# The low half of a reloaded weight piece, given to VectorE one unit later

## The chip, the cores and the metric

One core of one Trainium2 chip runs the whole program, one launch. The metric is device time in microseconds (us) of one execution; lower is better.

## What is computed

Three blocks follow one another, all in 32-bit floats. First attention over 2 x 8 heads of 768 tokens with 64 columns, in which a query sees only keys of its own hash bucket:

```python
q_bits = (np.einsum('bhsd,dk->bhsk', q, proj) > 0).astype(np.int64)
k_bits = (np.einsum('bhsd,dk->bhsk', k, proj) > 0).astype(np.int64)
...
mask = q_bucket[:, :, :, None] == k_bucket[:, :, None, :]
scores = np.where(mask, scale * np.matmul(q, k.transpose(0, 1, 3, 2)), -1000000000.0)
attn = np.exp(scores - np.max(scores, axis=-1, keepdims=True))
attn = attn / (np.sum(attn, axis=-1, keepdims=True) + 1e-09)
return np.matmul(attn, v).astype(np.float32)
```

Then a gated feed-forward block, `((x @ w1) * (x @ w2)) @ w3 @ w_out` on 1536 tokens of 512 columns (hidden width 1024), and at the end a layer of 8 experts, of which each token uses the one with the largest gate logit: `gate * (relu(x @ w1[e]) @ w2[e])`.

## The kernel before

The matmuls want more precision than one pass gives, so most operands are held as two numbers, a high part (rounded by a copy on ScalarE) and a low part (the rest, a subtraction on VectorE or GpSimd), and three products are summed (`TERMS`). The high part must be there before the low part can be taken.

The attention is written as a loop over units, `for i in range(NU + LEAD + NLAG + 1)` with `NU` = 96, and the order of the instructions of every engine is the order in which the loop emits them. Unit i does, in this order: `stage_1(units[i])` for i under 96 (two score matmuls, L343, and the row maximum of these scores on VectorE, L350, read from PSUM); the transpose of the finished maxima when a half is complete (`stage_f`, L361, with a copy `rT` on ScalarE and two small writes by SP, L366); whatever was put off to this unit (`todo_at`, filled by `after(n, fn)`, run at L861); `stage_a`, the product with v (L392); `stage_2` for unit i - 9 (four score matmuls, L378, the exponential on ScalarE, L379, and the running sum of the exponentials on GpSimd, `acc`, L384); from unit 98 on half a feed-forward step of the next block (`moe_half`, L682); and at the very end of the unit `flush()`, which emits what lies in `misc`. `stage_1` and `stage_2` draw their PSUM tiles from one tag, `s`, with two buffers; which of the two a tile gets is settled when the program is built, and a tile's first matmul waits until the buffer's last reader is through. A unit from 92 on also begins with `norm_step` (`x_t`'s high part by a ScalarE copy, L638, and its low part by VectorE one unit later, L640).

The weights w1 and w2 were written to DRAM earlier, as 16 pieces of 128 x 512 (`wfd`), and come back from unit 84 on through a ring of five buffers, `st`. In `order` they have the numbers k = 40 to 55. A piece is split by `split`: ScalarE copies its high part to `hi` (L494) and VectorE subtracts, `lo = T - hi` (L495). For k from 40 on, both are emitted by `flush()` at the end of the unit, followed by `nxt()`, which asks for the load of piece k + 5 into the same buffer two units later (`after(2, ...)`, L467 on SP). By `RATE2` the pieces 40 to 45 are flushed in the units 91 to 96, one each, 46 and 47 in unit 97, 48 to 53 in the units 98 to 103, and 54 and 55 in unit 104. The first `moe_half`, in unit 98, reads the high and the low parts of the pieces 40, 42, 44 and 46.

Of the kernel before, what the change touches and what calls it, by code (L numbers as in the profile page):

```python
# [8 lines left out]
F32 = mybir.dt.float32  # L9
# [31 lines left out]
READY = 84  # L41
NST = 5
LEAD = 9
NDVE = 0
AGE = 2
NLAG = 4
RUN = 2
# [118 lines left out]
def body(tc, qT, kT, vP, w1d, w2d, w3d, wod, mod, wgate, mbias, e1, e2, cst, out):  # L166
    nc = tc.nc
    PE, ACT, DVE, POOL, SP = nc.tensor, nc.scalar, nc.vector, nc.gpsimd, nc.sync
# [28 lines left out]
    def ps(tag, shape, name):  # L197
        return psum[0].tile(shape, F32, tag=tag, name=name, bufs=nbuf.get(tag, 1))
# [248 lines left out]
    dq, misc, begun = [], [], set()  # L447

    def piece_load(k):
        i = order[k]  # L450
        if k in raws:
            return
        if i < 8:
            src = wod[i * P:(i + 1) * P, :]
        elif i < 24:
            f, hf = divmod(i - 8, 2)
            src = w3d[f, :, hf * 4:hf * 4 + 4, :].rearrange("p g f -> p (g f)")
        else:
            m, j = divmod((i - 24) % 16, 8)
            c, hf = divmod(j, 2)  # L460
            src = ((w1d, w2d)[m] if i < 40 else wfd[m])[c * P:(c + 1) * P, hf * 512:hf * 512 + 512]
        if i < 40:
            raws[k] = r_cr([P, 1024])
            SP.dma_start(raws[k].bitcast(I64), src)
        else:
            raws[k] = r_st([P, 512])
            SP.dma_start(raws[k], src)  # L467

    def piece(k):
        i = order[k]  # L470
        raw = raws[k]
        if i < 8:
            hi, lo = wo[:, 0, i, :], wo[:, 1, i, :]
        elif i < 24:
            f, hf = divmod(i - 8, 2)
            if hf == 0:
                w3_t[f] = r_w3([P, 2, 8, P], F32R)
            hi, lo = (w3_t[f][:, x, hf * 4:hf * 4 + 4, :].rearrange("p g f -> p (g f)") for x in range(2))
        elif i >= 40:
            m, j = divmod(i - 40, 8)  # L480
            c, hf = divmod(j, 2)
            hi, lo = (w12[m][:, x, c, hf * 512:hf * 512 + 512] for x in range(2))

        def nxt():
            ahead = k + (3 if k < 40 else NST)
            if ahead < (40 if k < 40 else 56):
                if k < 40:
                    piece_load(ahead)
                else:
                    after(2, lambda: piece_load(ahead))  # L490
            done["n"] += 1

        def split(T):
            ACT.copy(hi, T)  # L494
            (POOL if NDVE <= k < 40 else DVE).tensor_sub(lo, T, hi.bitcast(F32))  # L495

        if i >= 40:
            return [lambda: misc.append(lambda: (split(raw), nxt()))]
        T, t1 = r_T([P, 512]), ps("u", [P, 512], f"u{k}").bitcast(I32)
        w = raw.bitcast(I32).rearrange("p (n two) -> p n two", two=2)  # L500

        def last():
            DVE.scalar_tensor_tensor(T.bitcast(I32), w[:, :, 0], 29, t1, ALU.logical_shift_right, ALU.bitwise_or)
            if i < 24:
                misc.append(lambda: (split(T), nxt()))
            else:
                m, j = divmod(i - 24, 8)
                c, hf = divmod(j, 2)
                SP.dma_start(wfd[m][c * P:(c + 1) * P, hf * 512:hf * 512 + 512], T)
                misc.append(nxt)  # L510

        return [
            lambda: DVE.tensor_scalar(t1, w[:, :, 1], 3, 0x3FFFFFF8, ALU.logical_shift_left, ALU.bitwise_and),
            lambda: DVE.scalar_tensor_tensor(t1, w[:, :, 1], -0x40000000, t1, ALU.bitwise_and, ALU.bitwise_or),
            last,
        ]

    def fill():
        if dq and isinstance(dq[0], int):
            dq[0:1] = piece(dq[0])  # L520
        if dq:
            dq.pop(0)()
# [42 lines left out]
    def after(n, fn):  # L565
        todo_at.setdefault(slot[0] + n, []).append(fn)
# [567 lines left out]
    for i, k in enumerate((1, 2, 4, 8)):  # L1134
        nxt = inc[i % 2]
# [410 lines left out]
```

## Time and profile before

| | |
|---|---|
| runs | 687.93, 692.60, 692.66 us; median 692.6 |
| the profiled execution, its own time | 686.77 us |
| its span in the profile | 685.0 us |
| TensorE busy (matmul) | 653.3 us, 95% of the span |
| VectorE, ScalarE, GpSimd busy | 391.7, 313.2, 329.4 us |
| granted TensorE clock | 0.998 |

The profile is of one execution, with times counted from the start of its span; 1.8 us of the execution's time lie outside of it. PE is TensorE's matmul, DVE is VectorE, ACT is ScalarE, POOL is GpSimd, and SP issues the DMAs. L350 is line 350 of the kernel. In a timeline, what stands in brackets is the engine's idle time ahead of the row and the work whose end finished it.

### The profile page before, as it was taken

What the parts mean: (1) busy time and instruction counts of PE and PEld (TensorE: products, weight loads), DVE (VectorE), ACT (ScalarE), POOL (GpSimd) and SP (SyncE); (2) the same over time, 40 slices, a digit from 0 to 9 for tenths busy, and PEclk for the clock granted to TensorE, in tenths of its full rate; (3) what the DMA queues carried; (4) which work ended last, traced back from release to release, by engine and by line L of the source; (5) the groups of instructions that cost most, each with busy time, mean ns of one, the idle gap of its engine ahead of it and who ended that gap; (6) DMA issues with size and microseconds to landing.
All of it is one profiled execution on the core that took longest, in us unless ns stands there. A gap on an engine that the chain in (4) does not pass through costs nothing. (4 is left out here: it accounts for less than half of the span.)

```text
span 685.0 us, 11038 instructions
## 1 busy us (share of the span) xinstructions
PE 653.3 (95%) x4038; PEld 512.0 (75%) x4038; DVE 391.7 (57%) x606; ACT 313.2 (46%) x534; POOL 329.4 (48%) x323
## 2 busy tenths in 40 slices
PE   7998899999999897899999999999999999999995
PEld 2544666676667654578989898989888899899984
DVE  6788768676786997753632121121275775575550
ACT  7266474655555544553422122221224665565551
POOL 7499987787768576665524233231215222111110
PEclk9999999999999999999999999999999999999999
DMA  8747372736557555303201010100036887766630
GB/s 223 229 147 212 126 236 87 228 139 161 168 149 200 147 190 159 100 32 96 65 17 47 16 47 16 47 1 32 1 119 235 288 293 237 243 198 218 203 121 20
DMA packets 41692, 94.04 MB, mean 137 GB/s; under 512 B 6352, under 2 KB 12032, under 8 KB 41632
## 3 DMA queue, kind: packets, MB, share of 16 engines
q1 hardware_dynamic: 39552, 86.72, 40.9%
q0 software_dynamic: 2080, 6.56, 2.7%
q8 instruction: 34, 0.56, 0.3%
q14 instruction: 26, 0.21, 0.1%
HBM read 72.98 MB, written 12.94 MB: 125 GB/s over the span
## 5 line engine op out<-in xcount | busy, mean ns | idle before, releaser
L682 PEld LDWEIGHTS ab<-x,w 128*128 128x128 f32 x1152 | 140.5, 191 | 7.9 <-DVE w L495 2.4
L682 PE MATMUL ab<-x,w 128*128 128x256 f32 x1152 | 143.9, 284 | 2.6 <-DVE w L495 1.6
L384 POOL TENSOR_TENSOR acc<-acc,pt 128x770 f32<-128x770 f32 x64 | 119.4, 1865 | 17.6 <-ACT pt L379 12.4
L379 ACT ACTIVATE pt<-s 128x768 f32<-128x768 f32 x96 | 78.0, 813 | 97.3 <-PE s L378 89.9
L350 DVE TENSOR_REDUCE nm<-m 128x1 f32<-128x768 f32 x96 | 91.3, 954 | 52.6 <-PE m L343 52.4
L378 PEld LDWEIGHTS s<-q,k 128*128 128x128 f32 (+1 forms) x384 | 64.0, 189 | 42.4 <-issue 20.2
L693 POOL TENSOR_TENSOR g<-gf,g 128x256 fp32r<-128x256 f32 x48 | 35.3, 736 | 124.8 <-ACT g L692 119.4
L378 PE MATMUL s<-q,k 128*128 128x384 f32 (+1 forms) x384 | 91.5, 360 | 2.2 <-ACT pt L379 1.2
L1212 DVE TENSOR_TENSOR eu<-er,eu 128x1024 fp32r<-128x1024 f32 x56 | 68.1, 1233 | 25.0 <-ACT eu L1211 23.8
L392 PE MATMUL a<-pt,v 128*64 128x385 f32 x384 | 76.5, 504 | 0.0
L1401 POOL DMA_INDIRECT out<-o,sidx x13 | 14.7, 1131 | 121.6 <-ACT o L1400 105.6
L691 DVE TENSOR_TENSOR gf<-asb,ab 128x256 f32<-128x256 f32 x48 | 20.2, 420 | 92.7 <-ACT asb L690 92.4
L1375 PE MATMUL e1F<-ex,eu 128*128 128x256 f32 x576 | 70.3, 283 | 0.5 <-DVE ex L1341 0.3
L1375 PEld LDWEIGHTS e1F<-ex,eu 128*128 128x128 f32 x576 | 69.8, 190 | 1.4 <-DVE ex L1341 0.5
L1393 PE MATMUL e2F<-eu,h 128*128 128x512 f32 x288 | 69.0, 395 | 0.1
L1211 ACT CAST eu<-er 128x1024 fp32r<-128x1024 f32 x56 | 57.6, 1046 | 10.2 <-DMA er<-e 10.1
L1393 PEld LDWEIGHTS e2F<-eu,h 128*128 128x128 f32 x288 | 53.2, 188 | 11.6 <-DVE h L1380 0.5
L343 PE MATMUL m<-k,q 78*128 78x384 f32 x192 | 51.9, 353 | 10.0 <-DVE nm L350 6.8
L1011 PE MATMUL x2p<-w,g 128*128 128x512 f32 x240 | 58.1, 396 | 0.0
L596 PE MATMUL w<-wo,w 128*128 128x512 f32 x192 | 51.3, 400 | 1.9 <-ACT ev L599 1.6
L1011 PEld LDWEIGHTS x2p<-w,g 128*128 128x128 f32 x240 | 44.2, 188 | 11.4 <-issue 2.1
L690 ACT COPY asb<-ab 128x256 f32<-128x256 f32 x48 | 17.9, 372 | 72.2 <-PE ab L682 72.2
(202 smaller groups left out, 810.7 us busy)
## 6 DMA issues: line engine op xcount, KB each, us to landing
er<-e SPq DMA_DIRECT2D x56, 512.0 KB
cr<-w3d SPq DMA_DIRECT2D x16, 512.0 KB
cr<-wod SPq DMA_DIRECT2D x8, 512.0 KB
cr<-w1d SPq DMA_DIRECT2D x8, 512.0 KB
wfd<-cT SPq DMA_DIRECT2D x16, 256.0 KB
cr<-w2d SPq DMA_DIRECT2D x8, 512.0 KB
st<-wfd SPq DMA_DIRECT2D x16, 256.0 KB
raw<-kT SPq DMA_DIRECT2D x8, 384.0 KB
```

What stands on the lines that cost most here:

```text
L343: PE.matmul(s[:, half, 0:HS], q[0:KROWS[hd], 0, qt * P:qt * P + P], k[0:KROWS[hd], 0, half * HS:half * HS + HS], start=True, stop=True,)
L350: DVE.tensor_reduce(nm[:, 3 * hd + qt % 3:3 * hd + qt % 3 + 1], s[:, :, 0:HS], AX.XY, ALU.max, negate=True)
L378: PE.matmul(s[:, hd, 0:HS], k[0:n, i, c * P:c * P + P], q[0:n, i, cl], start=(i == 0), stop=(i == 1))
L379: ACT.activation(pts[j % NP][:, :, 0:HS], s[:, :, 0:HS], AF.Exp, scale=SCALE)
L384: POOL.tensor_add(acc, pts[(j - 1) % NP] if c == 1 else acc, pts[j % NP])
L392: PE.matmul(a_t[p, half][64 * hd:64 * hd + 64, :], v[:, c, 64 * hd:64 * hd + 64], pts[j % NP][:, hd, :], start=(c == 0), stop=(c == QT - 1 ...
L682: PE.matmul(ab[:, j, :], w12[j][:, st, c, fs], x[:, mv, c, :], start=(c == 0 and i == 0), stop=(c == 3 and i == 2))
L1011: PE.matmul(st["ps"], g_t[ch][:, a, f, i * P:i * P + P], w34[b][:, f, :], start=(f == 0 and k == 0), stop=(f == 7 and k == 2),)
L1211: ACT.copy(t[:, 0, sl], raw)
L1212: DVE.tensor_sub(t[:, 1, sl], raw, t[:, 0, sl].bitcast(F32))
L1375: PE.matmul(o[f], w[:, st, c, fs], x[:, mv, c, :], start=(c == 0 and i == 0), stop=(c == 3 and i == 2))
L1393: PE.matmul(o, h[:, st, f, sl], w[:, mv, f, :], start=(f == 0 and k == 0), stop=(f == 7 and k == 2))
```

## The change

For the pieces with k from 40 on, only the ScalarE copy is still emitted at the end of the unit. The VectorE subtraction, and behind it `nxt()`, go through `after(1, ...)`, so they are emitted in the next unit, behind `stage_1` and `stage_f` of that unit and ahead of its `stage_a`. `nxt()` counts its two units from there, so the request for the next load is emitted one unit later too. The constant `NDVE` goes, and the earlier pieces stay with GpSimd as before.

```diff
-NDVE = 0
...
         def split(T):
             ACT.copy(hi, T)
-            (POOL if NDVE <= k < 40 else DVE).tensor_sub(lo, T, hi.bitcast(F32))
+            POOL.tensor_sub(lo, T, hi.bitcast(F32))
 
         if i >= 40:
-            return [lambda: misc.append(lambda: (split(raw), nxt()))]
+            def later():
+                DVE.tensor_sub(lo, raw, hi.bitcast(F32))
+                nxt()
+
+            return [lambda: misc.append(lambda: (ACT.copy(hi, raw), after(1, later)))]
```

## Rows read from the trace of the kernel before

**Rows 1.** Page, busy time of each engine, with share and instructions.

```profile
PE 653.3 (95%) x4038; PEld 512.0 (75%) x4038; DVE 391.7 (57%) x606; ACT 313.2 (46%) x534; POOL 329.4 (48%) x323
```

**Rows 2.** Five stretches: length, busy us of each engine, PE clock, DMA share, GB/s.

```profile
core 0: us, PE busy (x) PEld busy (x) DVE busy (x) ACT busy (x) POOL busy (x), PEclk, DMA share, GB/s
263.86:285.64 21.78, 16.71 (x86) 8.72 (x85) 16.49 (x16) 13.33 (x24) 13.34 (x11) 1.00 0.36 98
276.31:278.80 2.49, 2.38 (x16) 0.84 (x14) 2.21 (x4) 2.04 (x5) 1.01 (x3) 1.00 0.36 105
285.95:309.00 23.05, 23.05 (x150) 17.32 (x150) 13.08 (x13) 12.07 (x23) 13.02 (x10) 1.00 0.17 58
309.00:520.00 211.00, 210.00 (x1523) 189.76 (x1522) 70.01 (x202) 54.80 (x135) 68.87 (x92) 1.00 0.15 47
520.00:670.00 150.00, 149.37 (x955) 134.53 (x955) 89.21 (x115) 82.90 (x126) 27.58 (x25) 1.00 0.67 226
```

**Rows 3.** Timeline of PE, units 92 to 98: start, duration, engine, line, tiles.

```profile
263.86 0.51 PE L343 MATMUL m<-k,q 78*128 78x384 f32 x2
...
266.96 0.62 PE L343 MATMUL m<-k,q 128*128 128x384 f32 x2 [0.90 <-ACT pt L379]
...
270.61 0.62 PE L343 MATMUL m<-k,q 78*128 78x384 f32 x2 [1.26 <-DVE nm L350]
...
273.89 0.62 PE L343 MATMUL m<-k,q 128*128 128x384 f32 x2 [0.96 <-ACT pt L379]
...
279.07 0.28 PE L361 MATMUL f<-ident,nm 128*12 128x128 f32 x1 [0.38 <-POOL nm L357]
...
285.64 0.38 PE L682 MATMUL ab<-x,w 128*128 128x256 f32 x1 [1.56 <-DVE w L495]
```

**Rows 4.** Timeline of VectorE, units 91 to 98.

```profile
265.61 1.85 DVE L495 TENSOR_TENSOR w<-st,w 128x512 fp32r<-128x512 f32 x1 [2.69 <-ACT w L494]
267.38 0.95 DVE L350 TENSOR_REDUCE nm<-m 128x1 f32<-128x768 f32 x1
268.25 1.44 DVE L495 TENSOR_TENSOR w<-st,w 128x512 fp32r<-128x512 f32 x1
269.61 0.94 DVE L350 TENSOR_REDUCE nm<-m 128x1 f32<-128x768 f32 x1
270.80 0.69 DVE L495 TENSOR_TENSOR w<-st,w 128x512 fp32r<-128x512 f32 x1 [0.24 <-ACT w L494]
271.41 0.42 DVE L640 TENSOR_TENSOR x<-xT,x 128x256 fp32r<-128x256 f32 x1
...
276.55 0.94 DVE L350 TENSOR_REDUCE nm<-m 128x1 f32<-128x768 f32 x1
...
281.27 2.07 DVE L640 TENSOR_TENSOR x<-xT,x 128x256 fp32r<-128x256 f32 x1
283.27 2.32 DVE L495 TENSOR_TENSOR w<-st,w 128x512 fp32r<-128x512 f32 x1
```

**Rows 5.** Timeline of GpSimd, the running sums of the units 91, 92 and 95 to 98.

```profile
265.07 4.07 POOL L384 TENSOR_TENSOR acc<-acc,pt 128x770 f32<-128x770 f32 x2 [1.60 <-ACT pt L379]
...
278.98 8.29 POOL L384 TENSOR_TENSOR acc<-acc,pt 128x770 f32<-128x770 f32 x4
```

**Rows 6.** Timeline of ScalarE, units 92, 98 and 99.

```profile
266.10 0.81 ACT L379 ACTIVATE pt<-s 128x768 f32<-128x768 f32 x1 [0.52 <-PE s L378]
...
283.59 0.61 ACT L494 CAST w<-st 128x512 fp32r<-128x512 f32 x1
287.82 0.81 ACT L379 ACTIVATE pt<-s 128x768 f32<-128x768 f32 x1 [3.61 <-PE s L378]
```

**Rows 7.** Timeline of SP's DMA issues, units 95 to 98.

```profile
276.31 0.32 SPq L467 DMA_DIRECT2D st<-wfd  x1
...
280.28 1.40 SPq L366 DMA_DIRECT2D q<-rT  x2
281.78 0.34 SPq L467 DMA_DIRECT2D st<-wfd  x1
```

## The prediction

> **What bounds the kernel now.** The engines' busy times come first: TensorE has 653.3 us of work in a span of 685.0, every other engine under 400 [rows 1]. So only a change that shortens TensorE's idle time counts, and the table by stage says where it idles. From the unit 92 to the first feed-forward half in unit 98 it works 16.71 of 21.78 us, so 5.07 us are lost; behind that it works 23.05 of 23.05, then 210.00 of 211.00 and 149.37 of 150.00 [rows 2]. A microsecond won before 285.95 us is therefore not waited away later: nothing there shows an end that another engine or a DMA sets.
>
> The timeline of PE names the five places [rows 3]: the scores of unit 93 wait 0.90 us for an exponential, those of unit 94 wait 1.26 for a maximum, those of unit 95 wait 0.96 for an exponential, the transpose of the maxima waits 0.38 for GpSimd, and the first half step waits 1.56 for the low part of piece 46. Together 5.06. The reader should see that three of them come from one cause, which stands on VectorE [rows 4]. The scores of unit 92 are ready at 263.86 + 0.51 = 264.37, but ahead of their maximum stands the subtraction of piece 40, for whose high part VectorE idles 2.69 us; it ends at 267.46, and the maximum runs only at 267.38. The same goes on: the maximum of unit 93 stands behind the subtraction of piece 41, which ends at 269.69. A late maximum keeps its PSUM buffer. That the scores of the units 93 and 95 wait for an exponential means that they were given the other buffer of the two, the one that `stage_2` has just used; the exponential of unit 92 ends at 266.10 + 0.81 = 266.91 [rows 6], and the scores of 93 start at 266.96.
>
> **The change, part by part.** Nothing is added or taken away: the same 16 copies, 16 subtractions and 11 loads run. What differs is the order on two queues.
>
> VectorE. The order changes for few pieces only. There is no maximum after unit 95, so only the subtractions of pieces 40 to 43 (flushed in the units 91 to 94) move behind one. Those of 42 to 45 also move behind one L640, 0.42 us where nothing disturbs it [rows 4]. From piece 46 on, no VectorE instruction stands between the old place and the new one: cost nothing, gain nothing. The maximum of unit 92 then starts at 264.4 and ends at 265.4, since it takes 0.95; the subtraction of 40 starts where it did, as its high part comes no sooner. So the scores of unit 93 can follow the matmuls of unit 92 directly, at about 265.9 in place of 266.96. I take it that the tile gets the buffer that comes free first, which is now the maximum's; the other case is a rival below. The maximum of 93 follows the subtraction of 40 at 267.4 and ends at 268.4, where it ended at 270.55; the scores of 94 start at about 268.4 in place of 270.61. By the same steps those of 95 start at about 271.1 in place of 273.89. Of the three waits, 3.12 us, I leave 0.2 for 94 and 0.4 for 95: 2.5 us won. The 0.38 at the transpose goes as well if the last maximum leads the additions by enough; I count between 0 and 0.4. TensorE thus reaches the half step 2.5 to 2.9 us sooner.
>
> The 1.56 us there are the doubtful term. Behind the last maximum (276.55 + 0.94 = 277.49) VectorE now has five subtractions up to piece 46, which ends at 285.59 [rows 4]; with the change it has six, because piece 43 moves behind that maximum. What one costs depends on GpSimd: undisturbed 0.69, but 1.85 at 265.61 and 2.32 at 283.27, each while a running sum was under way, and four sums back to back took 8.29, that is 2.07 each [rows 4, 5]. The 1.85 fit a sum that began at 265.07 and left VectorE its turn only after it. The Trainium skill, page "SBUF — State Buffer", section "Who interferes with whom", states it as a rule: a VectorE instruction with two SBUF inputs and a GpSimd instruction that reads SBUF exclude one another for the whole instruction, and whichever starts first goes first. The trace agrees: 2.07 for an L640 that takes 0.42 alone. By that rule the moved subtractions are no dearer in themselves, but each that meets a sum waits for its end; without it six subtractions would take the 0.69 or 0.42 of an undisturbed one and the 1.56 would be gone.
>
> So I follow the chain with one subtraction let in per sum. The last maximum ends between 273.0 (L640 ahead of it runs at once) and 274.8 (it waits for a sum of 1.8). Three or four subtractions fit before the sums of unit 95 and later begin, and one or two must pass between sums. Piece 46 then ends between 280.3 (soonest, by its copy on ScalarE) and 283.8. VectorE's own work in the stretch, 16.49 us from 264.4 on, gives 280.9 as a floor [rows 2]. TensorE wants it at 284.08 less 2.5 to 2.9, so about 281.4. The gain at 285.64 is then between 1.8 and 4.2 us; with the middle, 282.6, it is 3.0, and I take that.
>
> SP. The load of piece k + 5 is emitted a unit later, but an issue waits on its buffer, not on the unit: the load goes out when the subtraction of piece k is done. It matters only where something else on SP's queue comes between. The load of piece 45 now stands behind the two loads of `rb`, which wait for nothing new: nothing. The load of piece 48 stood ahead of the two rT writes (276.31) and now stands behind them, as that of 49 does before, at 281.78 [rows 7]. Its data needed 2.49 us, 105 GB/s over the stretch, which is its 0.26 MB [rows 2]. Shifted 3 us with the rest it goes out at about 278.8 and lands at 281.3; its copy ran at 283.59 and would now be due at about 280.6. So ScalarE may stand 0.7 us, and what is queued behind it is an exponential that waited 3.61 us for its scores [rows 6]: hidden. If that cover were gone it would cost 0.7. The `st` ring counts as empty one unit later, in unit 106 in place of 105, and the buffer that needs its room is first drawn in unit 107: nothing.
>
> ScalarE's order is the same, and so is GpSimd's. The sum: 2.5 to 2.9 from TensorE's waits, 0.1 to 0.5 from the half step, so 3.0. Against the profiled execution, 686.77 becomes 683.8 (span 682.0); it ran 5.8 us under the median of the runs, so on the median the forecast is 692.6 - 3.0 = 689.6 us.
>
> **Rivals.** (1) The tile keeps the exponential's buffer. Then the scores of 93 still start at 266.96, and of the three waits only the one on the maximum goes, 1.26 us, the rest being paid at the half step: 692.6 - 1.3 = 691.3. For it: the assignment before has it so at two of three units. Against it: the maximum would now be the earlier reader by 1.5 us. (2) The half step swallows all. Its wait ends with piece 46, and if the six subtractions take as long as the five did and the copy time that was idle, that end stays at 285.6: 692.6. For it: VectorE is busy 16.49 of 21.78 us there, more than ScalarE [rows 2]. Against it: its largest gap, 2.69, is exactly what the change fills. (3) Slower. The sixth subtraction falls into the row of sums, and all six have to wait for one: 6 x 2.07 = 12.4 us behind the last maximum. The point is 285.6 - 12.4 = 273.2: if that maximum ends later, the half step starts later than before. At 274.8 this costs 1.6 us, at the old 277.5 it costs 4.3; with the middle, 3.0, the time is 695.6. Against it: the sums resume at 278.98, 1.5 us behind the last maximum [rows 4, 5], which is room for two undisturbed subtractions. (4) All 5.06 go, 687.5, if the sums and the subtractions happen to miss each other.
>
> **How the numbers follow.** Forecast 0.60, rival (1) 0.17, (2) 0.10, (3) 0.08, (4) 0.05. The runs shown lie 4.7 us apart, 0.7%, so about 1% is what a measurement of this kernel can tell from no change. No case moves the time by 1%: 3.0 us are 0.4%, 4.3 are 0.6%. So faster by over 1% needs the gain and a median that falls among the lower runs, 0.11; slower by over 1% needs rival (3) and the reverse, 0.05; within 1% is 0.84. The range goes from 683, the profiled execution less 3 and a little, since a median may as well fall there, to 694, which takes in (1), (2) and the low end of (3).
>
> **What would show it.** In the profile after: the maximum of unit 92 at about 264.4, before the subtraction of piece 40, and no 2.69 us gap ahead of the latter; scores of the units 93 to 95 with less than 0.7 us of waits together; the first half step's wait for L495 between 0 and 2.4 us; work as without gaps behind it. The prediction is wrong if a wait of `stage_2` for a PSUM buffer takes the place of those of `stage_1`, if exponentials begin to wait for the running sums, or if a later stage shows new TensorE gaps.

## The result

| | median (lowest to highest) | runs | profiled: time, span, clock |
|---|---|---|---|
| before | 692.63 (687.93 to 694.10) | 4 | 686.77, 685.0, 0.998 |
| changed | 682.73 (680.84 to 682.87) | 4 | 682.61, 680.8, 0.995 |

The changed kernel takes 0.986 of the time of before, interval 0.9818 to 0.9903: faster by 1.4%, under the range that was given. The two profiled executions, however, differ by 4.2 us only, the medians by 9.9. Both have to be explained.

The stage from the scores of unit 92 to the end of the first half step, after the change (length, busy us of each engine, PE clock, DMA share, GB/s), and the stretches behind it:

```profile
265.10:281.88 16.78, 16.25 (x87) 8.89 (x86) 13.23 (x16) 12.84 (x23) 12.51 (x10) 1.00 0.32 90
281.88:309.00 27.12, 26.12 (x175) 19.56 (x175) 15.60 (x16) 13.84 (x27) 16.14 (x12) 1.00 0.23 72
309.00:520.00 211.00, 211.00 (x1520) 190.64 (x1520) 69.66 (x199) 53.65 (x132) 69.25 (x92) 1.00 0.16 50
520.00:670.00 150.00, 149.46 (x954) 135.01 (x953) 89.78 (x114) 84.87 (x129) 24.13 (x23) 1.00 0.67 221
```

TensorE is idle 0.53 us there, where it was 5.07 [rows 2]. From the start of unit 92's scores to the matmul behind the half step it takes 16.78 us, against 285.95 - 263.86 = 22.09 before [rows 2, 3]: 5.3 us less. Idle time makes 4.5 of it. The other 0.8 stands in the profile as busy time: a wait costs a little more than its bracket says, as the first matmuls behind one take longer (the scores of unit 93 took 0.62 us behind a wait and take 0.51 without; the last matmul of the half step took 0.38 [rows 3], where 12 in a row now take 1.60). Behind the stage TensorE works as without gaps as it did (the 1.00 us that was missing between 309 and 520, a wait for ScalarE, now falls before 309). The profiles differ by less than 5.3 because this execution reached unit 92 1.24 us later, for a reason that comes below.

The timeline of PE after, at the five places of [rows 3]:

```profile
265.10 0.51 PE L342 MATMUL m<-k,q 78*128 78x384 f32 x2
...
267.14 0.51 PE L342 MATMUL m<-k,q 128*128 128x384 f32 x2
...
269.63 0.62 PE L342 MATMUL m<-k,q 78*128 78x384 f32 x2 [0.27 <-DVE nm L349]
...
272.21 0.62 PE L342 MATMUL m<-k,q 128*128 128x384 f32 x2 [0.26 <-DVE nm L349]
...
276.84 0.27 PE L360 MATMUL f<-ident,nm 128*12 128x128 f32 x1
...
280.35 1.60 PE L685 MATMUL ab<-x,w 128*128 128x256 f32 x12
```

Waits of 0.90, 1.26, 0.96, 0.38 and 1.56 us have become none, 0.27, 0.26, none and none. The 12 matmuls of the half step stand in one row. VectorE, for [rows 4]:

```profile
265.64 0.96 DVE L349 TENSOR_REDUCE nm<-m 128x1 f32<-128x768 f32 x1 [1.50 <-PE m L342]
266.84 1.86 DVE L498 TENSOR_TENSOR w<-st,w 128x512 fp32r<-128x512 f32 x1 [0.24 <-ACT w L501]
268.63 0.94 DVE L349 TENSOR_REDUCE nm<-m 128x1 f32<-128x768 f32 x1
269.50 1.46 DVE L498 TENSOR_TENSOR w<-st,w 128x512 fp32r<-128x512 f32 x1
...
276.58 0.42 DVE L643 TENSOR_TENSOR x<-xT,x 128x256 fp32r<-128x256 f32 x1
278.45 0.79 DVE L498 TENSOR_TENSOR w<-st,w 128x512 fp32r<-128x512 f32 x1 [1.45 <-ACT w L501]
280.25 3.49 DVE L498 TENSOR_TENSOR w<-st,w 128x512 fp32r<-128x512 f32 x2 [1.01 <-ACT w L501]
```

and GpSimd's row of running sums, for [rows 5]:

```profile
276.68 8.77 POOL L383 TENSOR_TENSOR acc<-acc,pt 128x770 f32<-128x770 f32 x4
```

The maximum of unit 92 now runs 0.54 us behind the start of its scores, ahead of the subtraction of piece 40, whose idle time has shrunk from 2.69 to 0.24 us. And there is something that the prediction had not: L643, which was L640, takes 0.42 us at 276.58 where it took 2.07 [rows 4]. It no longer stands behind the subtraction of piece 45, which still waits 1.45 us for its high part, and it starts 0.10 us before the row of running sums does, at 276.68.

### The profile page after: what moved, and what is told of

Same layout as the page of the kernel before. It is cut to its first block, busy times and chain, and to the rows that moved or that the text cites. A ratio compares the mean times of both kernels' runs of the same rounds, so it can differ in the third digit from the quotient of the medians.

```text
span 680.8 us, 11038 instructions
## 1 busy us (share of the span) xinstructions
PE 652.6 (96%) x4038; PEld 513.0 (75%) x4038; DVE 388.8 (57%) x606; ACT 313.6 (46%) x534; POOL 328.4 (48%) x323
```

## The experiments

14 kernels were run. The first four were to settle whether the whole median is explained by the five waits, and by which of the two queues.

**The two kernels again**, no edit.

> The kernel before once more, unchanged, timed against itself. Theory A (the change is worth what the profiles of the units 92 to 98 show, about 5 us; the four runs of before that lay at 692 to 694 are the chip's own scatter): the ratio is 1.00, the times scatter over some 5 us again, from 687 to 693, with no common reason. Theory B (in most of its runs the kernel before pays a second price, TensorE's clock being granted at less than full somewhere): runs near 692 show a mean granted clock of 0.99 or less, runs near 687 show 0.998, and a profile of a slow one shows a stretch below 1.00.

> The changed kernel once more. Both theories: 680 to 683 us, each 0.001 of granted clock worth about 0.7 us (0.001 x 680). Theory A: against before on the same chip 5 us less (ratio 0.993) once runs of equal clock are compared. Theory B: 10 us less (0.986), 5 of them at a higher clock.

Before, against itself: 687.28 us (686.11 to 694.80, 12 runs), ratio 0.9986 (0.995 to 1.0023), with five runs over 692 at clocks of 0.985 to 0.988, and six under 686.6 at 0.997 or 0.998. Changed: 681.28 us (680.62 to 684.04, 6 runs), ratio 0.989 (0.9846 to 0.9933). The profile was of a run of 694.80 us. Its table by stage, then its timeline of PE:

```profile
264.00:272.00 8.00, 6.09 (x28) 3.09 (x28) 5.29 (x5) 4.22 (x8) 5.00 (x3) 1.00 0.19 65
272.00:280.00 8.00, 6.79 (x20) 3.57 (x20) 5.20 (x7) 2.81 (x6) 1.82 (x1) 0.58 0.43 109
280.00:289.00 9.00, 7.96 (x46) 4.29 (x44) 6.95 (x5) 6.55 (x12) 7.58 (x8) 0.99 0.26 86
289.00:297.00 8.00, 6.38 (x23) 4.75 (x25) 2.77 (x3) 0.96 (x2) 1.01 (x1) 0.59 0.32 100
```

```profile
270.02 0.97 PE L378 MATMUL s<-q,k 78*128 78x384 f32 x4
272.25 0.62 PE L343 MATMUL m<-k,q 78*128 78x384 f32 x2 [1.26 <-DVE nm L350]
272.80 1.06 PE L392 MATMUL a<-pt,v 128*64 128x385 f32 x4
273.80 1.65 PE L378 MATMUL s<-q,k 78*128 78x384 f32 x4
276.41 1.01 PE L343 MATMUL m<-k,q 128*128 128x384 f32 x2 [0.96 <-ACT pt L379]
...
288.40 0.38 PE L682 MATMUL ab<-x,w 128*128 128x256 f32 x1 [0.82 <-DVE x L640]
290.62 0.58 PE L682 MATMUL ab<-x,w 128*128 128x256 f32 x1 [1.83 <-DVE w L495]
...
294.06 2.76 PE L682 MATMUL ab<-x,w 128*128 128x256 f32 x12
```

The waits at the scores are the same three. The one at the transpose is gone, and the half step now waits twice, 0.82 us for L640 and 1.83 for the low part of piece 46. What is new is the granted clock: it falls twice, once behind the waits at the scores and once behind those at the half step, to the lower level: 1.2 in place of 2.4 GHz, 0.50 in the single microseconds from 274 to 280 and from 291 to 297. Four score matmuls go from 0.97 to 1.65 us, a half step of 12 from 1.60 to 2.76. Theory B holds: the kernel before pays its waits twice in some runs. The profile that the prediction was made from was of a run without that.

**Each half of the change alone.** `sub_only`, then `load_only`:

```diff
             def later():
                 DVE.tensor_sub(lo, raw, hi.bitcast(F32))
-                nxt()
...
-            return [lambda: misc.append(lambda: (ACT.copy(hi, raw), after(1, later)))]
+            return [lambda: misc.append(lambda: (ACT.copy(hi, raw), after(1, later), nxt()))]
```

```diff
-            def later():
+            def first():
+                ACT.copy(hi, raw)
                 DVE.tensor_sub(lo, raw, hi.bitcast(F32))
-                nxt()
+                after(1, nxt)
...
-            return [lambda: misc.append(lambda: (ACT.copy(hi, raw), after(1, later)))]
+            return [lambda: misc.append(first)]
```

> Only VectorE's order of the change: the subtraction goes a unit later, the request for the next load stays where it was, so SP's order is that of before. Theory A1 (all of the gain is VectorE's order): the same as the changed kernel, within 1 us, and no TensorE wait on L350 or on an exponential over 0.3 us in the units 93 to 95. Rival A2 (the loads' later place has a part, as the two loads of rb leave earlier): 1 us or more slower than the changed kernel.

> Only SP's order of the change: the subtraction stays at the end of its unit, ahead of the next maximum, and the load request goes a unit later. Theory A1: the time of before (ratio 1.00), with the same five TensorE waits of 5 us in the units 92 to 98. Rival A2: 1 us or more faster than before.

The subtraction alone: 681.50 us (680.78 to 682.81, 6 runs), as the changed kernel. The loads alone: 687.71 (686.05 to 694.86, 12 runs), ratio 0.9986 (0.9949 to 1.0024), the three waits at the scores at 0.90, 1.27 and 0.96 us, and the clock down to 0.50 again. All of the gain is VectorE's order.

**Which pieces.** `first_four` puts off the subtraction only for `k < 44`, `last_twelve` only for `k >= 44`, `only_45` only for `k == 45`:

```diff
-            return [lambda: misc.append(lambda: (ACT.copy(hi, raw), after(1, later)))]
+            if k < 44:
+                return [lambda: misc.append(lambda: (ACT.copy(hi, raw), after(1, later)))]
+            return [lambda: misc.append(lambda: (ACT.copy(hi, raw), later()))]
```

> The change for the pieces 40 to 43 alone, whose subtraction moves behind a maximum; the others are subtracted at the end of their unit as before. Theory A1 (the maxima are what counts): within 0.7 us of the changed kernel, 681 to 682. Rival A3 (the order among the subtractions of pieces 44, 45 and L640 ahead of the half step has a part): 683 or more, with a wait for L495's work at the first half step.

> The change for the pieces 44 to 55 alone, where no maximum is left to pass. Theory A1: the times of before, 686 at best, with runs of 690 to 694 among them, and the same five TensorE waits. Rival A3: 684 or less at best, the wait at the half step shorter than 1 us.

> The change for piece 45 alone: on VectorE one pair changes places, the subtraction of piece 45 and the L640 of unit 97; the three waits at the scores stay. Theory A3 (in the kernel before, that L640 stands ready behind a subtraction that idles for its high part, and so falls into the running sums and takes 2.07 us, which the half step then waits for): 684.1 at best, as with the last twelve, L640 at 0.41 to 0.42, no wait at the half step, and no clock below full behind 285. Rival A4 (what won in the last twelve was the place of piece 44): 686 at best.

The first four: 682.93 at best, 684.03 in the median of 12. Theory A1 falls: the waits at the scores are down to 0.27 us, but the one at the half step is 1.69 us. The last twelve: 684.10 at best, 686.08 in the median; piece 45 alone: 684.24 and 685.50. Without a maximum being passed, that saves some 1.7 us at best. (Runs at a clock of 0.990 or less are still among these, three of 12 and two of 12, where the kernel before has nearly four in ten; so few runs can't tell these shares apart.) TensorE at the half step and VectorE in `first_four`, in the order of before:

```profile
282.03 0.38 PE L687 MATMUL ab<-x,w 128*128 128x256 f32 x1 [1.69 <-DVE w L498]
```

```profile
276.95 0.79 DVE L498 TENSOR_TENSOR w<-st,w 128x512 fp32r<-128x512 f32 x1 [1.45 <-ACT w L503]
277.67 2.07 DVE L645 TENSOR_TENSOR x<-xT,x 128x256 fp32r<-128x256 f32 x1
279.66 5.15 DVE L498 TENSOR_TENSOR w<-st,w 128x512 fp32r<-128x512 f32 x3
```

and in `only_45`, where that L640 (here L645) and the subtraction ahead of it have changed places and nothing else has:

```profile
282.33 1.58 PE L687 MATMUL ab<-x,w 128*128 128x256 f32 x12
```

```profile
277.34 0.69 DVE L498 TENSOR_TENSOR w<-st,w 128x512 fp32r<-128x512 f32 x1 [0.17 <-ACT w L503]
277.95 0.75 DVE L645 TENSOR_TENSOR x<-xT,x 128x256 fp32r<-128x256 f32 x2
279.82 1.28 DVE L498 TENSOR_TENSOR w<-st,w 128x512 fp32r<-128x512 f32 x1 [1.12 <-ACT w L502]
```

In the first, L645 is ready but stands behind a subtraction that idles 1.45 us, and then meets the row of running sums: 2.07 us. In the second both L645 run back to back, 0.75 us together, and end at 278.70, just before the sums begin at 278.73; the half step has no wait. Rival A3, and its narrow form, that it is this one pair, are shown.

**The other PSUM buffers**, the changed kernel with the buffers of before, pinned:

```diff
+FLIPS = ((7, 3, 1), (7, 4, 1), (7, 5, 1))
...
+    turn = [0]
+
+    def side(stay=False):
+        turn[0] ^= not stay
+        return "sA" if turn[0] else "sB"
...
-        s = ps("s", [P, 2, 512], f"m{p}_{qt}_{hd}")
+        s = ps(side((p, qt, hd) in FLIPS), [P, 2, 512], f"m{p}_{qt}_{hd}")
...
-        s = ps("s", [P, 2, 512], f"s{p}_{half}_{c}")
+        s = ps(side(), [P, 2, 512], f"s{p}_{half}_{c}")
```

> The changed kernel with the PSUM buffers of the kernel before: the scores of units 93 and 95 get the buffer that the exponential of the unit ahead has read, pinned by two tags. If the buffer matters as the prediction's rival (1) has it: TensorE waits for exponentials of 0.5 to 1.0 us before units 93 and 95 come back, 1 to 2 us slower than the changed kernel at equal clock, 682 to 683 at best. If it doesn't: 680.7 at best.

683.63 us (683.23 to 685.08, 12 runs), 2.3 us over the changed kernel's, a little more than expected. The timeline of PE:

```profile
268.53 0.62 PE L349 MATMUL m<-k,q 128*128 128x384 f32 x2 [0.90 <-ACT pt L385]
...
273.86 0.62 PE L349 MATMUL m<-k,q 128*128 128x384 f32 x2 [0.96 <-ACT pt L385]
...
284.44 0.39 PE L692 MATMUL ab<-x,w 128*128 128x256 f32 x1 [0.95 <-DVE w L505]
```

The two waits for exponentials are back, and a wait at the half step with them. So rival (1) of the prediction would have cost this much; the program built from the change has the maximum's buffer at both places.

**TensorE's gaps filled**, in the kernel before with its own order and buffers, by matmuls of identity by identity whose results nobody reads. `fill_gaps` has all, `fill_scores` the first part, `fill_half` the second, `fill_exact` all, but 1, 2, 1 and 2:

```diff
+GAPS = {93: 2, 94: 3, 95: 2}
...
+            if i in GAPS:
+                busy(GAPS[i], "m")
             stage_1(units[i])
...
             for i, (st, mv) in enumerate(TERMS):
+                if (ch, f, j, c, i) == (0, 0, 0, 3, 2):
+                    busy(4, "m")
                 PE.matmul(ab[:, j, :], w12[j][:, st, c, fs], x[:, mv, c, :], ...)
```

> The kernel before, in its own order and with its own PSUM buffers, with idle matmuls (identity by identity, results unused) put into TensorE's gaps: 2, 3 and 2 ahead of the scores of units 93, 94 and 95, and 4 ahead of the last matmul of the first half step; each takes some 0.34 us. Theory C (TensorE's clock falls because of these gaps): the waits stay, so the best time stays at 686 to 687, but no run goes to 690 or more, the mean clock is 0.994 or better in every run, and the median is 3 us or more under that of before. Rival D (the clock falls for another reason, such as the chip's state): runs of 690 to 694 at a clock under 0.99 remain as often as before, near one in two.

> The kernel before with the idle matmuls ahead of the scores of units 93 to 95 alone. Theory C (each gap brings its own fall of the clock): no fall between 270 and 281, but still one behind the wait at the half step in some runs, so 686.3 to 687 at best and 689 to 690 in those, none over 691. Rival C2 (the gaps at the scores alone bring both falls): as with all gaps filled, 687 to 689.5.

> The kernel before with the idle matmuls in the first half step alone. Theory C: no fall of the clock behind the half step, but still one between 270 and 281 in some runs: 686.5 to 687 at best, 690 to 691 in those. Rival C2: runs up to 694 remain.

> As fill_gaps, the order and buffers of the kernel before, but with fillers about as long as the waits: 1, 2 and 1 idle matmuls (0.69 us each) ahead of the scores of units 93 to 95, 2 in the half step. Theory C: best time that of before, 686.0 to 686.5, no run at 690 or more, all clocks 0.994 or better, median 686.3 to 687.7; what is left to the changed kernel, 5 to 5.5 us, is then the waits, and what before's median has above it is the clock. Rival D: runs of 690 to 694 as often as before, four in ten.

| 12 runs each | median (lowest to highest) | runs at 690 or more | lowest clock |
|---|---|---|---|
| fill_gaps | 687.42 (687.23 to 689.41) | 0 | 0.994 |
| fill_scores | 686.97 (686.52 to 688.80) | 0 | 0.994 |
| fill_half | 686.95 (686.61 to 693.28) | 3 | 0.988 |
| fill_exact | 687.09 (686.02 to 687.70) | 0 | 0.995 |
| before, in all experiments | 687.86 (685.96 to 695.14), 115 runs | 43 | 0.985 |

(One run of before, of 906.13 us at a mean clock of 0.655, is left out of the table, and so is its clock; another, of 688.77 us, stands at 0.948 and is left out of the last column.) An idle matmul took 0.69 us, not the 0.34 that I had counted, so the first three fill more than the gap and are up to 1.2 us dearer at best. Theory C's forecast that `fill_gaps` would lower the median by 3 us or more missed: 687.42 against 687.64 for before beside it, which itself ran at 690 or more less often than I had expected. `fill_exact` is the clean one. Its table by stage and its timeline of PE:

```profile
264.00:289.00 25.00, 23.74 (x115) 13.20 (x114) 18.89 (x17) 13.54 (x25) 15.39 (x12) 1.00 0.33 96
289.00:297.00 8.00, 8.00 (x54) 5.90 (x52) 3.70 (x5) 4.71 (x9) 3.59 (x3) 1.00 0.34 106
```

```profile
270.14 1.45 PE L335 MATMUL busy<-ident 128*128 128x384 f32 x4
271.59 0.62 PE L351 MATMUL m<-k,q 78*128 78x384 f32 x2
...
284.86 1.45 PE L335 MATMUL busy<-ident 128*128 128x384 f32 x4
286.62 0.39 PE L692 MATMUL ab<-x,w 128*128 128x256 f32 x1 [0.30 <-DVE w L503]
```

The work waits as long as before: the scores of unit 94 and the last matmul of the half step start 0.98 us later than in the profile of before (271.59 and 286.62 against 270.61 and 285.64 [rows 3]), and this execution was 0.96 us late already at the scores of unit 92, ahead of all fillers. The best time is that of before, 686.02 against 685.96. But none of 12 runs reaches 690, where 43 of 115 of before do, all of those at a clock of 0.990 or less. The three kernels with filled gaps at the scores have no such run in 36; `fill_half`, which has the same pinned buffers but not these fillers, has three in 12, so the pins are not what takes them away. Theory C is shown in this: it is TensorE's idling in these places that brings the lower clock. In the median that is little: `fill_exact` has a ratio of 0.9972 to before (0.9945 to 1.0). `fill_scores` speaks for the gaps at the scores as the ones that matter: with these filled, the wait of 1.56 us at the half step brought no run to 690. That is rival C2's forecast, not C's. But `first_four`, whose only long wait there is the half step's, shows 0.66 between 282 and 287:

```profile
282.00:287.00 5.00, 4.97 (x23) 4.11 (x23) 2.81 (x2) 1.02 (x2) 1.66 (x1) 0.66 0.61 196
```

Which gap brings which fall is not settled.

**A place that the change leaves.** The changed kernel has a fall of the clock itself, in some of its runs, and the kernel before has the same one. The timeline of PE of the changed kernel, and one microsecond of its table:

```profile
70.90 0.93 PE L377 MATMUL s<-q,k 78*128 78x384 f32 x4 [2.31 <-DMA q<-rT]
```

```profile
74.00:75.00 1.00, 1.00 (x4) 0.63 (x3) 0.58 (x1) 0.48 (x1) 1.00 (x2) 0.50 0.00 0
```

It follows a wait of 2.31 us for the maxima's write by DMA, in unit 27, and with that wait, longer than the 0.86 us of the execution profiled before, it is why unit 92 was reached later. That wait differs from execution to execution. In the profiles of the kernels that leave it unfilled, this fall stands behind waits of 1.76 and of 2.31 to 2.64 us (six profiles), and not behind waits of 0.73 to 1.98 (eight). Two kernels put idle matmuls ahead of `stage_2`, the first of them at a unit that I had counted wrongly:

```diff
-            if i == LEAD:
-                busy(4, "m")
+            if i in (LEAD, 21):
+                busy(4, "m")
```

```diff
-            if i == LEAD:
-                busy(4, "m")
+            if i in (LEAD, 27):
+                busy(4 if i == LEAD else 2, "m")
```

> The changed kernel with four idle matmuls more, 1.4 us, ahead of the exponentials' scores of unit 21, where TensorE waits 0.7 to 2.6 us for the maxima's write by DMA and the clock fell behind that in some runs of either kernel. Theory C: no fall at 70 to 80 us, every run within 680.5 to 681.7, median 0.3 us or more under the changed kernel's. Rival D: the same spread as the changed kernel, 680.6 to 684.

> The changed kernel with two idle matmuls, 1.4 us, ahead of the exponentials' scores of unit 27, where TensorE waits for the maxima's write by DMA. Theory C: no fall of the clock at 70 to 80 us, all runs between 680.5 and 681.5. Rival D: the spread of the changed kernel, 680.6 to 684. If the wait isn't there, the fillers cost 1.4 us: 682.

In unit 21: 682.62 us, 682.46 to 682.67. The fillers missed the wait and cost 1.8 us at best; no run of six has a clock under 0.996, and the later wait for the DMA is gone from the profile. In unit 27 they take its place, as the timeline of PE shows:

```profile
68.54 1.45 PE L332 MATMUL busy<-ident 128*128 128x384 f32 x4
70.14 0.94 PE L377 MATMUL s<-q,k 78*128 78x384 f32 x4
```

680.91 us (680.53 to 682.84, 6 runs), ratio to before 0.9895 (0.9856 to 0.9933). Five of six lie within 0.5 us and none has a clock under 0.996; the sixth, 682.84, has 0.998, so something else took its 2 us, which was not found. Against the changed kernel's 681.28, measured on another chip, this is no difference that these runs can tell. That it beats the change isn't shown.

## Why the prediction was wrong

**What was right.** The bound, the five places, and the order: the maximum first, the maximum's buffer, 0.2 and 0.4 us left at the scores of 94 and 95 (0.27 and 0.26 measured), the wait at the transpose gone, the work behind without gaps. SP's queue cost nothing, as `sub_only` shows. Its one stall was sized too small but hidden as said: ScalarE waits 1.59 us, not 0.7, for the load of piece 48, and TensorE has no wait from that. The timeline of ScalarE after:

```profile
283.04 0.62 ACT L501 CAST w<-st 128x512 fp32r<-128x512 f32 x1 [1.59 <-DMA st<-wfd]
283.75 0.81 ACT L378 ACTIVATE pt<-s 128x768 f32<-128x768 f32 x1
```

**The first step that failed** is the term for the half step, "0.1 to 0.5" of 1.56 us. The half step took 1.53 us (281.88 - 280.35) where it took 3.36 (285.95 - 282.59), so it gained 1.8. Its first matmuls before:

```profile
282.59 1.48 PE L682 MATMUL ab<-x,w 128*128 128x256 f32 x11
```

I counted a sixth subtraction behind the last maximum and a dearer chain, and wrote of the pieces 42 to 45, as a price, that they also move behind one L640 of 0.42. For piece 45 that is the gain: its L640 no longer stands behind an idle subtraction and is spared 1.65 of its 2.07 us. Piece 46 then ends at 281.5, 16.4 behind the start of unit 92's scores, which is the soonest that the prediction had (280.3 - 263.86), set by the copy on ScalarE. The floor of 280.9 that I took from VectorE's 16.49 us was none: that busy time held the 1.65 and other time spent beside the sums, and over the stage it fell to 13.23. A smaller part of the miss lies in the other term: TensorE reached the half step 3.5 us sooner (15.25 behind the start of unit 92's scores in place of 18.73), not 2.5 to 2.9, for the brackets of the waits are not all that a wait costs.

Together the stage gained 5.3 us, not 3.0. That is near rival (4), to which I had given 0.05, and by a cause that `only_45` shows, not because sums and subtractions happened to miss each other. What I had not worked out is the margin: L643 starts 0.10 us ahead of the sums, and 0.11 in the profiles of `after_again` and of `sub_only`. The Trainium skill's rule on the shared ports (page "SBUF — State Buffer", section "Who interferes with whom") was read in one direction only, as a cost of what moves. The trace agrees with the rule, at 2.07 and at 0.42 us of the same subtraction; what it said for this change lay in which of two operations gets through before the sums begin.

**The second, larger for the median,** is the step from the profiled execution to the median. It ran 5.8 us under it; I carried that distance over unchanged and took the spread of the runs for what a measurement can't tell from no change. Most of it is the clock, and which runs were drawn. Of the 115 runs of before, the 36 at a mean clock of 0.997 or more have a median of 686.29 us, and the 43 at 690 or more stand at 0.985 to 0.990. Four of the changed kernel's ten runs have 0.997 or more, with a median of 681.05. At like clock the change is therefore worth 5.2 us (5.5 if the line is drawn at 0.996), as the stage says; over all runs, 687.86 to 681.91, it is 6.0; and in the runs of the result, where three of the four of before lay at 692 or more, 9.9. Some 4 of these 9.9 us are the luck of the draw. (The mean clock is a rough sign only: every profile also stands at 0.50 for its last microseconds, behind TensorE's last matmul, where it costs nothing. The profile of `after_again`, at 0.996 and 680.62 us, has no other fall.) The prediction counted what TensorE loses while it waits, and left out what it can lose behind that. The Trainium skill has the clock as a gate that passes all pulses or half of them by how busy the engine has been (page "TensorE: Matmul & The Clock Gate", section "What's actually happening"); the traces agree, with 1.00 and 0.50 as the levels and each fall behind idle time of TensorE. The profile that I read had 1.00 throughout the stage [rows 2]; only the spread of the runs could have told.

**The sum by its parts**, from the runs at 0.997 or more, against 686.29: the maxima (`first_four`, 683.14) 3.15 us, the pair at piece 45 (`only_45`, 684.61) 1.68, together 4.8 of 5.2. These are medians of six and of four runs.

## What to carry to other kernels

Where an in-order engine idles for the input of one operation, look at everything that stands ready behind it, not only at the operation that was meant to gain: here one subtraction of 0.4 us behind such a gap was worth 1.7 us. The busy time of an engine is no floor if part of it is time spent beside another engine. A gap of TensorE has a second price where the clock falls behind it, and one profile may not show it, so compare times and clocks of several runs before their spread is taken for noise. Idle matmuls in the gap tell the two prices apart.

## What the runs showed of the hardware

That the clock falls behind so little idling I had not expected: in the profile of `before_again` TensorE worked 6.09 of the 8 us from 264 to 272, no wait at the scores was longer than 1.3 us, and the clock fell at 273; in the profile of before it worked 5.84 of the same 8 us, and the clock stayed at 1.00. Nearly four runs of ten of before lie at 690 us or more, at a clock of 0.990 or less, with the same program; what decides between runs was not found. A fall behind which TensorE had work lasted 3.4 to 6.8 us. An idle matmul, 128x128 by 384 columns, stands in the trace as two rows, 0.69 us together, where the two score matmuls of a unit, of 384 columns each, take 0.51; why was not looked into.
